# The first weights of a fused attention and FFN kernel, loaded as rows of 1024 columns

## The chip, the cores and the metric

The kernel runs on one core of a Trainium2 chip. The core has TensorE (PE in the profile), VectorE (DVE), ScalarE (ACT), GpSimd (POOL) and SyncE (SP); 16 DMA engines move data between HBM and the on-chip memory SBUF, and matrix products land in the eight banks of PSUM. The metric is the device time of one execution in microseconds (us), as the median of several runs.

## The reference

Eight images of 576 positions, eight heads of 64. Each position sees those at most 32 away; the result of the attention goes through a feed-forward network (FFN) with the tanh form of gelu.

```python
# q, k, v: (8, 8, 576, 64); w_in: (512, 2048); w_out: (2048, 512); all float32
scores = (q @ k.transpose(0, 1, 3, 2)) / sqrt(64)
scores = where(abs(pos[:, None] - pos[None, :]) <= 32, scores, -1e9)
attn = softmax(scores)
x = (attn @ v).transpose(0, 2, 1, 3).reshape(4608, 512)
out = gelu_tanh(x @ w_in) @ w_out                     # (4608, 512)
```

## The kernel before

**Tiling.** The 4608 tokens are worked on as nine tiles of 512 (`t`). For each tile TensorE makes the first product (`ffn_in`): 16 blocks of 128 hidden columns (`n`), each the sum over four row blocks of 128 rows of w_in (`dc`), so 64 matmuls of 128x512 in float16. ACT makes gelu of each block as it leaves PSUM. The second product (`ffn_out`, for tile 0 `ffn_out_0`) sums over the 16 blocks. While tile t is in its products, the attention of image t + 1 is woven into the same instruction streams, step by step, by plans written out by hand (`PLAN_0` for tile 0: at matmul number 4 the scores of group 0, at 9 the turning of pair 1, and so on). Attention is done for pairs of heads (`g`, `pr`): scores, exponential, mask by a band, sums, the product with the values.

**Order.** Nothing is scheduled by a program: each engine runs its instructions in the order in which the kernel's text names them, and waits for semaphores in between. An instruction that waits holds back all that stand behind it on its engine. Loads are issued by SP in the order of the text.

**The beginning.** SP issues q and k of image 0, then its values v by heads (`v_of_pair(g)`: two heads each, 128 KB a head), then w_in, then q and k of image 1 with w_out between them, then the values of image 1. The weights come as float32 and are cast to float16 (`w_in16`, `w_out16`) by DVE, POOL and ACT. They pass through five buffers of 1 MB (`stage`, tag "stage"): the first takes image 0's values, four take w_in, and w_out takes them again one after the other as they come free.

w_in is loaded by quarters of 512 columns (`load_w_in(i, ...)`, L232): a quarter is 1 MB, 4 row blocks of 128 rows, and each row's piece is 512 columns, 2 KB. Quarter 0 comes as two row blocks, then one, then one, with the values of heads 6 and 7 ahead of the last two (L259 to L263); quarters 1 to 3 come as two row blocks each time (L264 to L267).

**Tile 0.** Once the attention of image 0 has its pairs 0 to 2 (`finish`, L815: the product with the values on PE, then a multiplication on DVE, L508, that writes `xT[:, g]`), the first product begins. Row block `dc` of the product needs `xT[:, dc]`, that is pair `dc`, so the fourth pair is finished between row blocks 1 and 2 (L835 to L847): quarter 0's four blocks with row blocks 0 and 1, pair 3, then row blocks 2 and 3. Quarter 0's casts are on POOL (row blocks 0 and 2) and ACT (1 and 3), those of quarters 1 to 3 on DVE (0 and 2) and POOL (1 and 3). Then `quarter(1)`, `quarter(2)` and `quarter(3)` follow (L867 to L882), each row block by row block over its four blocks. A block keeps a PSUM bank from its first matmul to its gelu: blocks 0 to 7 go to the banks D, O, x0, x1, S0 (two halves, each a bank) and S1 (two), and 8 to 15 to the same in turn.

Two smaller pieces stand among these. `band_out` (L307) builds the band mask in six copies on DVE, for use from image 1 on; it stands ahead of `quarter(3, 0, 1)`. `trans_pair(1, 0, ...)` (L881) turns q and k of image 1's first pair by eight transposes on PE, halfway through quarter 3, and copies them out of PSUM: QT on DVE (L357), KT on ACT (L358). After quarter 3 come the casts of w_out's first megabyte (L884: chunk 0 on DVE, 2, 3 and 1 on POOL) and `cast_early(1, 1, ...)` on DVE, and then the second product of tile 0.

Of the kernel before, what the change touches and what calls it, by code (L numbers as in the profile page):

```python
# [9 lines left out]
FP32 = mybir.dt.float32  # L10
FP16 = mybir.dt.float16
# [67 lines left out]
def kernel(  # L79
# [9 lines left out]
    nc = tc.nc  # L89
    B, H, S, D = q.shape  # L90
# [12 lines left out]
    def load_table(which):  # L103
        nc.scalar.add_instruction(mybir.InstLoadActFuncSet(  # L104
            name=nc.get_next_instruction_name(), act_func_set_id=which, ins=[], outs=[]))
# [9 lines left out]
    stage = ctx.enter_context(tc.tile_pool(name="stage", bufs=5))  # L115
    yp = ctx.enter_context(tc.tile_pool(name="yp", bufs=2))
    psM = ctx.enter_context(tc.tile_pool(name="psM", bufs=1, space=PSUM))
    psS = ctx.enter_context(tc.tile_pool(name="psS", bufs=1, space=PSUM))
    psO = ctx.enter_context(tc.tile_pool(name="psO", bufs=1, space=PSUM))
# [11 lines left out]
    w_in16 = big.tile([128, 4, DF], FP16, name="w_in16")  # L131
# [94 lines left out]
    w_in_v = moe_w_in.rearrange("(c p) f -> p c f", p=128)  # L226
    w_out_v = moe_w_out.rearrange("(c p) f -> p c f", p=128)

    def stage_w():
        return stage.tile([128, 4, 512], FP32, name="wst", tag="stage")  # L230

    def load_w_in(i, w, c0=0, c1=4):  # L232
        nc.sync.dma_start(w[:, c0:c1, :], w_in_v[:, c0:c1, 512 * i:512 * i + 512])
        return w

    def load_w_out(i, w, c0=0, c1=4):
        nc.sync.dma_start(w[:, c0:c1, :], w_out_v[:, 4 * i + c0:4 * i + c1, :])
        return w

    def cast_w(w, dst, on_dve=(0, 1), cs=range(4), on_act=()):  # L240
        for c in cs:
            (nc.scalar.copy if c in on_act else nc.vector.tensor_copy if c in on_dve else nc.gpsimd.tensor_copy)(
                dst[:, c, :], w[:, c, :])
# [8 lines left out]
    def v_of_pair(g, hs=(0, 1)):  # L252
        for h in (2 * g + x for x in hs):
            nc.sync.dma_start(raws[0][3][:, :, h, :], v[0, h, 0:512, :].rearrange("(c p) d -> p c d", p=128))  # L254

    vs(4)
    for g in range(3):
        v_of_pair(g)
    wi = [stage_w()]  # L259
    load_w_in(0, wi[0], 0, 2)  # L260
    for x in range(2):
        v_of_pair(3, (x,))
        load_w_in(0, wi[0], 2 + x, 3 + x)  # L263
    for i in range(1, 4):  # L264
        wi.append(stage_w())
        for c0 in (0, 2):
            load_w_in(i, wi[i], c0, c0 + 2)  # L267

    idle = KTs[1][:, 0, 0:512]
    nc.vector.memset(idle, 0.0)  # L270
# [19 lines left out]
    def blocks(copy, dst, src, r, *pieces):  # L290

        for p0, n, w, u in pieces:
            v0 = u + (8 if r == even else 24)
            copy(dst[r, :, p0:p0 + n * w].rearrange("k j (n p) -> k j n p", n=n),
                 src[r, :, v0:v0 + w].rearrange("k j (o p) -> k j o p", o=1).broadcast_to([64, 4, n, w]))
# [11 lines left out]
    def band_out():  # L307
        blocks(nc.vector.tensor_copy, band, full, even, (0, 1, 24, 8), (24, 3, 32, 0), (120, 1, 24, 0))
        blocks(nc.vector.tensor_copy, band, full, odd, (0, 1, 40, -8), (40, 2, 32, 0), (104, 1, 40, 0))
# [36 lines left out]
    def trans_pair(b, pr, pt, ptk=None, now=True, copy=nc.vector.tensor_copy):  # L346
        q16, k16 = halfs[b][0:2]
        ptk = pt[:, 4:8, :] if ptk is None else ptk
        for j in range(4):
            nc.tensor.transpose(pt[:, j, :], q16[:, pr, j, :, :], idn)  # L350
        for j in range(4):
            nc.tensor.transpose(ptk[:, j, :], k16[:, pr, j, :, :], idn)
        if now:
            trans_out(b, pr, pt, ptk, copy)

    def trans_out(b, pr, pt, ptk, copy=nc.vector.tensor_copy):
        nc.vector.tensor_copy(QTs[b][:, pr, :, 0:128], pt[:, 0:4, :])  # L357
        copy(  # L358
            KTs[b % 2][:, pr, :].rearrange("d (p j) -> d p j", j=4),
            ptk[:, 0:4, :].rearrange("d j p -> d p j"))  # L360

    def bank(i):

        return psM.tile([128, 512], FP32, name="mm", tag=f"x{i}")

    def bank16(i):
        return psM.tile([128, 8, 128], FP16, name="pt", tag=f"x{i}")
# [154 lines left out]
    def column(t, n):  # L522

        return n // 2 + 8 * (n % 2) if t else n

    def ffn_in(t, n, d0=0, d1=4, then=True):
        fc = column(t, n)
        if t not in gTs:
            gTs[t] = gp.tile([128, NF, 512], FP16, name="gT", tag="gT")
        if d0 == 0:  # L530
            if t == 0:
                i = n % 8
                if i in (4, 6):
                    phs["S"] = psS.tile([128, 2, 512], FP32, name="ph2", tag=f"S{i // 2 - 2}")
                phs[fc] = psO.tile([128, 512], FP32, name="ph", tag="DO"[i]) if i < 2 else \
                    bank(i - 2) if i < 4 else phs["S"][:, i % 2, :]
            else:
                i = 3 if n in (1, 2) else 0 if n == 0 else (2, 1, 0)[n % 3] if t < NT - 2 else (2, 0)[n % 2 if n > 3 else 0]
                if n == 1:
                    phs["S"] = psS.tile([128, 2, 512], FP32, name="ph3", tag="S0")  # L540
                phs[fc] = bank(i) if i < 2 else phs["S"][:, n - 1, :] if i == 3 else \
                    psO.tile([128, 512], FP32, name="ph", tag="D")
        ph = phs[fc]
        for dc in range(d0, d1):
            nc.tensor.matmul(ph, w_in16[:, dc, fc * 128:fc * 128 + 128],  # L545
                             xT[:, dc, t * 512 % RING:t * 512 % RING + 512],
                             start=(dc == 0), stop=(dc == 3))
        if d1 == 4 and then:
            gelu(t, n)

    def gelu(t, n):
        fc = column(t, n)
        nc.scalar.activation(gTs[t][:, fc, :], phs[fc], AF.Gelu_apprx_tanh)  # L553
        if t and n % 4 == 3:
            sums(t, n // 4)
# [98 lines left out]
    def sums(t, i, which=slice(0, 4)):  # L654

        g, r = gTs[t], slice(2 * i, 2 * i + 2)
        A11, A21, A12, A22 = (g[:, r0 + 2 * i:r0 + 2 * i + 2, c:c + 256]
                              for r0 in (0, 8) for c in (0, 256))
        S1, S2, S3, S4 = (wino[f"S{n}"][:, r, :] for n in (1, 2, 3, 4))
        for dst, x, y, op in ((S1, A21, A22, ALU.add), (S2, S1, A11, ALU.subtract),  # L660
                              (S3, A11, A21, ALU.subtract), (S4, A12, S2, ALU.subtract))[which]:
            nc.vector.tensor_tensor(dst, x, y, op=op)  # L662
# [109 lines left out]
    def pieces(tag, name):  # L772
        return psO.tile([128, 512], FP32, name=name, tag=tag) if tag in "OD" else \
            psS.tile([128, 2, 512], FP32, name=name, tag=tag)[:, 0, :]
# [35 lines left out]
    def values(g, copy):  # L810
        hs = slice(2 * g, 2 * g + 2)
        copy(Vs[0][:, 0:4, hs, :], raws[0][3][:, :, hs, :])
        pair_v(0, nc.vector.tensor_copy, hs)

    def finish(g, o):  # L815
        times(0, g, o, groups.pop((0, g)))
        spread(0, g, o, lts[g])
# [11 lines left out]
    s0 = psS.tile([128, 2, 512], FP32, name="ps_o", tag="S0")  # L829
# [1 line left out]
    sums_of(3)  # L831
    spin(2, 512, s0[:, 1, :])
    values(2, nc.gpsimd.tensor_copy)
    finish(2, s0[:, 0, :])
    nc.gpsimd.tensor_copy(w_in16[:, 0, 0:512], wi[0][:, 0, :])  # L835
    nc.scalar.copy(w_in16[:, 1, 0:512], wi[0][:, 1, :])
    values(3, nc.vector.tensor_copy)
    for dc in range(2):
        for n in range(4):
            ffn_in(0, n, dc, dc + 1)  # L840
    finish(3, pieces("S1", "ps_o"))
    load_table(gelu_set)
    nc.gpsimd.tensor_copy(w_in16[:, 2, 0:512], wi[0][:, 2, :])
    nc.scalar.copy(w_in16[:, 3, 0:512], wi[0][:, 3, :])
    for dc in range(2, 4):
        for n in range(4):
            ffn_in(0, n, dc, dc + 1)  # L847
    cast_w(wi[1], w_in16[:, :, 512:1024], (0, 2))
    cast_w(wi[2], w_in16[:, :, 1024:1536], (0, 2))
    wo.append(load_w_out(1, stage_w()))  # L850
    qk(4)
    tails_0("q")
# [11 lines left out]
    cast_open(1)  # L864
    split = (nc.gpsimd, nc.vector)

    def quarter(i, *dcs):  # L867
        for dc in dcs:
            for n in range(4 * i, 4 * i + 4):
                ffn_in(0, n, dc, dc + 1, then=False)  # L870
        if 3 in dcs:
            for n in range(4 * i, 4 * i + 4):
                gelu(0, n)

    quarter(1, 0, 1, 2, 3)
    cast_w(wi[3], w_in16[:, :, 1536:2048], (0, 2))
    quarter(2, 0, 1, 2, 3)
    cast_early(1, 0, split)
    band_out()
    quarter(3, 0, 1)  # L880
    trans_pair(1, 0, psO.tile([128, 8, 128], FP16, name="pt", tag="D"), bank16(0)[:, 0:4, :], copy=nc.scalar.copy)  # L881
    quarter(3, 2, 3)  # L882
    load_table(exp_set)
    cast_w(wo[0], w_out16[:, 0:4, :], (0,), (0, 2, 3, 1))  # L884
    cast_early(1, 1, (nc.vector, nc.vector))
# [8 lines left out]
    for t in range(NT):  # L894
# [56 lines left out]
        for i in range(113 if t else 65):  # L951
# [8 lines left out]
            for act in plan.get(i, "").split():  # L960
# [18 lines left out]
                elif kind in "np":  # L979
# [7 lines left out]
                    if kind == "n":  # L987
                        n = size(1, g)
# [85 lines left out]
```

## Time and profile before

| | |
|---|---|
| median of 3 runs | 299.17 us (298.62 to 299.78) |
| the profiled execution, its own time | 298.71 us |
| its span, first to last instruction | 297.0 us |
| PE busy | 287.1 us, 97% of the span |
| clock granted to PE | 0.999 of full speed |
| HBM read and written | 36.70 and 9.44 MB |
| w_in: loads and their issues | 4 MB in 9 issues on SP, issued from 11.35 us on |
| w_out: loads and their issues | 4 MB in 6 issues on SP, issued from 21.86 us on |

All places in time are microseconds from the first instruction of the profiled execution. The profile gives a page of totals, and a trace that can be asked for groups of instructions, for waits, for stages, and for each engine's instructions in order of time. A row of the last kind has the start, the duration, the engine, the line of the kernel, what is written from what, and in brackets the idle time before it and what ended it. PE's rows last longer than the distance from one matmul to the next, since matmuls are pipelined; where PE is full, the distance from start to start is what a matmul costs.

### The profile page before, as it was taken

How to read it: one execution, taken by the hardware profiler on the slowest of the kernel's cores; microseconds unless marked ns; L12 is line 12 of the kernel's file. 1: busy time of each engine (PE TensorE's matmuls, PEld its weight loads, DVE VectorE, ACT ScalarE, POOL GpSimd, SP SyncE). 2: the span in 40 equal slices, each digit the busy share in tenths (PEclk: the TensorE clock that was granted, in tenths of full speed). 3: DMA queues.
4: the chain of work that ended last, by engine and by line, in shares of the span. 5: the costliest groups of instructions: out<-in, count | busy, mean ns of one | idle time of the engine just before them, and what ended most of it. 6: DMA issues, size and time to landing. Idle time of an engine off the chain costs nothing.

```text
span 297.0 us, 7282 instructions
## 1 busy us (share of the span) xinstructions
PE 287.1 (97%) x2949; PEld 184.7 (62%) x2949; DVE 209.2 (70%) x466; ACT 196.4 (66%) x315; POOL 89.4 (30%) x141
## 2 busy tenths in 40 slices
PE   7889999999999999999999999999999999999993
PEld 3534444446874587458844884488547867786783
DVE  4662475997986676868686879576966776964772
ACT  4876756778587876678657965695669557705800
POOL 3435415201407731406080606060800050015000
PEclk9999999999999999999999999999999999999999
DMA  7999999989999998989997997999594040004013
GB/s 216 263 297 383 366 280 263 264 178 202 291 192 191 235 233 156 145 167 244 150 193 116 253 145 158 142 227 170 102 175 38 0 116 29 2 13 131 0 35 109
DMA packets 116615, 51.01 MB, mean 172 GB/s; under 512 B 98391, under 2 KB 110167, under 8 KB 116582
## 3 DMA queue, kind: packets, MB, share of 16 engines
q1 hardware_dynamic: 91684, 38.67, 61.6%
q0 software_dynamic: 23776, 10.83, 23.0%
q10 hardware_dynamic: 1122, 1.06, 1.1%
q8 instruction: 23, 0.38, 0.6%
q14 instruction: 10, 0.08, 0.1%
HBM read 36.70 MB, written 9.44 MB: 155 GB/s over the span
## 4 chain that ended last, share of the span: by engine, by line
PE 80%; DMA 13%; DVE 2%; SPq 2%; ACT 1%; issue 1%; POOL 0%
PE mm L719 32%; PE mm L545 17%; PE ph L545 15%; DMA wst<-in_moe_w_out_dram 7%; DMA wst<-in_moe_w_in_dram 5%; PE pu L597 3%; PE ps_s L436 3%; PE ps_d L463 2%; DMA tr<-in_k_dram 2%; PE ps_o L473 2%; SPq L254 2%; PE mm L597 1%; PE ps_od L473 1%; PE ps_od L463 1%; PE mm L691 1%; PE py L719 1%
## 5 line engine op out<-in xcount | busy, mean ns | idle before, releaser
L545 PEld LDWEIGHTS <-w_in 128*128 128x128 f16 x512 | 49.7, 98 | 56.9 <-POOL w_in L835 0.5
L545 PE MATMUL ph<-xT,w_in 128*128 128x512 f16 x256 | 64.1, 379 | 0.4 <-POOL w_in L835 0.4
L545 PE MATMUL mm<-xT,w_in 128*128 128x512 f16 x256 | 64.1, 379 | 0.0
L681 POOL DMA_DIRECT2D out_dram<-y x55 | 32.3, 597 | 83.8 <-DVE y L748 75.5
L553 ACT ACTIVATE gT<-mm 128x512 f16<-128x512 f32 x60 | 35.6, 598 | 33.1 <-PE mm L545 32.5
L719 PEld LDWEIGHTS <-s 128*128 128x128 f16 x512 | 49.3, 98 | 7.1 <-DVE s L662 0.6
L719 PE MATMUL mm<-t,s 128*128 128x256 f16 x376 | 45.2, 273 | 0.3 <-DVE y L732 0.2
L662 DVE TENSOR_TENSOR s<-gT 128x512 f16<-128x512 f16 x64 | 27.2, 426 | 19.0 <-ACT gT L553 18.8
L719 PEld LDWEIGHTS <-gT 128*128 128x128 f16 x384 | 36.2, 98 | 6.5
L553 ACT ACTIVATE gT<-ph 128x512 f16<-128x512 f32 x58 | 32.2, 600 | 10.9 <-PE ph L545 10.9
L449 ACT ACTIVATE pe<-ps_s 128x960 f16<-128x960 f32 (+1 forms) x31 | 29.5, 974 | 13.9 <-PE ps_s L436 13.8
L719 PE MATMUL mm<-w_out,gT 128*128 128x256 f16 x256 | 32.6, 273 | 0.0
L104 ACT ACT_TABLE_LOAD x18 | 23.1, 1283 | 2.2 <-issue 1.9
L498 ACT ACTIVATE lt<-ps_d 128x480 f32<-128x480 f32 (+2 forms) x28 | 15.6, 556 | 10.4 <-PE ps_d L463 6.9
L499 ACT ACTIVATE lt<-lt 128x480 f32<-128x480 f32 (+3 forms) x36 | 21.1, 585 | 1.1
L458 DVE TENSOR_TENSOR pe<-pe,band 128x960 f16<-128x960 f16 x28 | 18.6, 683 | 2.3 <-ACT pe L449 2.3
L473 PEld LDWEIGHTS <-V 128*64 128x64 f16 x520 | 13.8, 111 | 6.3 <-DVE V L218 1.2
L719 PE MATMUL mm<-t,gT 128*128 128x256 f16 x128 | 16.1, 273 | 0.0
L208 POOL DMA_DIRECT2D V<-in_v_dram x16 | 14.3, 909 | 1.1 <-POOL after L953 0.4
L662 DVE TENSOR_TENSOR s<-s,gT 128x512 f16<-128x512 f16 x32 | 13.9, 434 | 1.1
L719 PE MATMUL mm<-w_out,s 128*128 128x256 f16 x120 | 14.6, 273 | 0.0
L508 DVE TENSOR_TENSOR xT<-ps_o,lt 128x480 f16<-128x480 f32 (+5 forms) x26 | 13.4, 536 | 1.1 <-PE ps_o L473 1.1
(146 smaller groups left out, 387.1 us busy)
## 6 DMA issues: line engine op xcount, KB each, us to landing
kr<-in_k_dram SPq DMA_DIRECT2D x31, 256.0 KB, 10.0
qr<-in_q_dram SPq DMA_DIRECT2D x6, 1024.0 KB, 6.9
wst<-in_moe_w_in_dram SPq DMA_DIRECT2D x7, 512.0 KB, 8.4
wst<-in_moe_w_out_dram SPq DMA_DIRECT2D x2, 1024.0 KB, 11.6
wst<-in_moe_w_out_dram SPq DMA_DIRECT2D x4, 512.0 KB, 5.8
qr<-in_v_dram SPq DMA_DIRECT2D x8, 256.0 KB, 5.6
V<-in_v_dram POOLq DMA_DIRECT2D x16, 128.0 KB, 8.8
qr<-in_q_dram SPq DMA_DIRECT2D x7, 256.0 KB, 6.9
```

The source lines that it names most:

```text
L104: nc.scalar.add_instruction(mybir.InstLoadActFuncSet(name=nc.get_next_instruction_name(), act_func_set_id=which, ins=[], outs=[]))
L208: nc.gpsimd.dma_start(V[:, c, :, :], v[b, :, 128 * c:128 * c + 128, :].rearrange("h p d -> p h d"))
L449: nc.scalar.activation(pe, ps[:, :, 0:w], AF.Exp, scale=SCALE)
L458: nc.vector.tensor_tensor(pe, pe, m.rearrange("k (o j) p -> k o j p", o=1).broadcast_to(list(pe.shape)), op=ALU.mult)
L473: nc.tensor.matmul(o[64 * h:64 * h + 64, cols].rearrange("d (j p) -> d j p", j=4)[:, :, p0 - q0:p1 - q0], Vs[b % 2][:, slot, 2 * pr + h, : ...
L498: nc.scalar.activation(lt[:, 0:n], d[:, 0:n], AF.Ln)
L499: nc.scalar.activation(lt[:, 0:n], lt[:, 0:n], AF.Exp, scale=-1.0)
L545: nc.tensor.matmul(ph, w_in16[:, dc, fc * 128:fc * 128 + 128], xT[:, dc, t * 512 % RING:t * 512 % RING + 512], start=(dc == 0), stop=(dc = ...
L553: nc.scalar.activation(gTs[t][:, fc, :], phs[fc], AF.Gelu_apprx_tanh)
L662: nc.vector.tensor_tensor(dst, x, y, op=op)
L681: eng.dma_start(out_v[b, j, q0 + p:q0 + p + e, cols], yo[m:m + e, cols])
L719: nc.tensor.matmul(pys["apart"][:, 0:256] if apart else py[:, blk, :], lhsT, wino[w][:, f, :], start=(new and i % (8 if one else 16) == 0) ...
```

## The change

w_in is loaded as eight pieces of one row block and 1024 columns, so that each of the 128 rows is 1024 columns long, 4 KB. `x` is the half of the columns, `dc` the row block; the order is row blocks 0 and 1 of the left half, with the values of heads 6 and 7 behind the first and the second, then row blocks 2 and 3, and then the right half. Two row blocks share one buffer of 1 MB. The casts are still of 128x512, two to each load: row blocks 0 and 1 of the left half on POOL and ACT, 2 and 3 on POOL and DVE, the right half on DVE and POOL.

The first product of tile 0 follows that order: blocks 0 to 5 with row block 0, then with row block 1, then pair 3 of the attention, then row blocks 2 and 3; then block 6, block 7, blocks 8 to 13 row block by row block, block 14, and block 15. Gelu follows directly on a block's last matmul. Pairs 2 and 3 of the attention leave PE through the two halves of S1, as S0 is now a bank pair of blocks 4 and 5.

`band_out` moves ahead of the casts of the right half. The turned pair moves from the middle of the last quarter to between blocks 14 and 15; its queries now use bank x0 and its keys bank D, and the copy of KT is on DVE in place of ACT.

```diff
+    wi = {}
+
+    def load_w_in(x, dc):
+        if dc % 2 == 0:
+            wi[x, dc // 2] = stage.tile([128, 2, 1024], FP32, name="wst", tag="stage")
+        nc.sync.dma_start(wi[x, dc // 2][:, dc % 2, :], w_in_v[:, dc, 1024 * x:1024 * x + 1024])
+
+    def cast_w_in(x, dc, *copies):
+        for y, copy in enumerate(copies):
+            copy(w_in16[:, dc, 1024 * x + 512 * y:1024 * x + 512 * y + 512],
+                 wi[x, dc // 2][:, dc % 2, 512 * y:512 * y + 512])
...
-    wi = [stage_w()]
-    load_w_in(0, wi[0], 0, 2)
     for x in range(2):
+        load_w_in(0, x)
         v_of_pair(3, (x,))
-        load_w_in(0, wi[0], 2 + x, 3 + x)
-    for i in range(1, 4):
-        wi.append(stage_w())
-        for c0 in (0, 2):
-            load_w_in(i, wi[i], c0, c0 + 2)
+    for x, dc in ((0, 2), (0, 3), (1, 0), (1, 1), (1, 2), (1, 3)):
+        load_w_in(x, dc)
...
     values(2, nc.gpsimd.tensor_copy)
-    finish(2, s0[:, 0, :])
-    nc.gpsimd.tensor_copy(w_in16[:, 0, 0:512], wi[0][:, 0, :])
-    nc.scalar.copy(w_in16[:, 1, 0:512], wi[0][:, 1, :])
+    s1 = psS.tile([128, 2, 512], FP32, name="ps_o", tag="S1")
+    finish(2, s1[:, 0, :])
+    six = range(6)
+
+    def block_in(ns, *dcs):
+        for dc in dcs:
+            for n in ns:
+                ffn_in(0, n, dc, dc + 1)
+
+    cast_w_in(0, 0, nc.gpsimd.tensor_copy, nc.scalar.copy)
     values(3, nc.vector.tensor_copy)
-    for dc in range(2):
-        for n in range(4):
-            ffn_in(0, n, dc, dc + 1)
-    finish(3, pieces("S1", "ps_o"))
+    block_in(six, 0)
+    cast_w_in(0, 1, nc.gpsimd.tensor_copy, nc.scalar.copy)
+    block_in(six, 1)
+    finish(3, s1[:, 1, :])
     load_table(gelu_set)
-    nc.gpsimd.tensor_copy(w_in16[:, 2, 0:512], wi[0][:, 2, :])
-    nc.scalar.copy(w_in16[:, 3, 0:512], wi[0][:, 3, :])
-    for dc in range(2, 4):
-        for n in range(4):
-            ffn_in(0, n, dc, dc + 1)
-    cast_w(wi[1], w_in16[:, :, 512:1024], (0, 2))
-    cast_w(wi[2], w_in16[:, :, 1024:1536], (0, 2))
+    cast_w_in(0, 2, nc.gpsimd.tensor_copy, nc.vector.tensor_copy)
+    cast_w_in(0, 3, nc.gpsimd.tensor_copy, nc.vector.tensor_copy)
+    block_in(six, 2, 3)
+    band_out()
+    for dc in range(4):
+        cast_w_in(1, dc, nc.vector.tensor_copy, nc.gpsimd.tensor_copy)
...
-    quarter(1, 0, 1, 2, 3)
-    cast_w(wi[3], w_in16[:, :, 1536:2048], (0, 2))
-    quarter(2, 0, 1, 2, 3)
+    for n in (6, 7):
+        block_in((n,), 0, 1, 2, 3)
+    block_in(range(8, 14), 0, 1, 2, 3)
     cast_early(1, 0, split)
-    band_out()
-    quarter(3, 0, 1)
-    trans_pair(1, 0, psO.tile([128, 8, 128], FP16, name="pt", tag="D"), bank16(0)[:, 0:4, :], copy=nc.scalar.copy)
-    quarter(3, 2, 3)
+    block_in((14,), 0, 1, 2, 3)
+    pt = psO.tile([128, 8, 128], FP16, name="pt", tag="D")
+    trans_pair(1, 0, bank16(0)[:, 0:4, :], pt[:, 0:4, :])
+    block_in((15,), 0, 1, 2, 3)
```

More of the change, by code (lines that the diff above doesn't have):

```diff
@@ L230, in stage_w @@
         return stage.tile([128, 4, 512], FP32, name="wst", tag="stage")
-    def load_w_in(i, w, c0=0, c1=4):
-        nc.sync.dma_start(w[:, c0:c1, :], w_in_v[:, c0:c1, 512 * i:512 * i + 512])
-        return w
+    wi = {}
[7 more added lines that the diff above has]
+                 wi[x, dc // 2][:, dc % 2, 512 * y:512 * y + 512])
     def load_w_out(i, w, c0=0, c1=4):
@@ L865 @@
     split = (nc.gpsimd, nc.vector)
[L867 to L873, printed above, removed]
-    quarter(1, 0, 1, 2, 3)
-    cast_w(wi[3], w_in16[:, :, 1536:2048], (0, 2))
-    quarter(2, 0, 1, 2, 3)
+    for n in (6, 7):
+        block_in((n,), 0, 1, 2, 3)
+    block_in(range(8, 14), 0, 1, 2, 3)
     cast_early(1, 0, split)
-    band_out()
-    quarter(3, 0, 1)
-    trans_pair(1, 0, psO.tile([128, 8, 128], FP16, name="pt", tag="D"), bank16(0)[:, 0:4, :], copy=nc.scalar.copy)
-    quarter(3, 2, 3)
+    block_in((14,), 0, 1, 2, 3)
+    pt = psO.tile([128, 8, 128], FP16, name="pt", tag="D")
+    trans_pair(1, 0, bank16(0)[:, 0:4, :], pt[:, 0:4, :])
+    block_in((15,), 0, 1, 2, 3)
     load_table(exp_set)
```

## The prediction

> **What bounds the kernel now.** I read the page's busy times first, then the stages, then TensorE's (PE's) waits, then the order of time around each wait.
>
> The page, first part, its line of totals:
>
> ```profile
> PE 287.1 (97%) x2949; PEld 184.7 (62%) x2949; DVE 209.2 (70%) x466; ACT 196.4 (66%) x315; POOL 89.4 (30%) x141
> ```
>
> PE is busy for 287.1 of 297.0 us. The table by stage (PE, PEld, DVE, ACT, POOL busy us and counts; granted clock; DMA share; GB/s) shows where the other 10 us lie:
>
> ```profile
> 10.00:18.00 8.00, 6.47 (x134) 3.50 (x133) 5.17 (x13) 7.55 (x13) 3.66 (x6) 1.00 1.26 256
> 18.00:34.00 16.00, 15.35 (x89) 6.91 (x90) 6.81 (x20) 9.70 (x18) 6.93 (x10) 1.00 1.02 360
> 34.00:47.00 13.00, 12.49 (x129) 5.86 (x130) 7.68 (x16) 9.78 (x16) 4.52 (x7) 1.00 1.11 306
> 47.00:57.00 10.00, 9.49 (x123) 4.78 (x123) 8.22 (x17) 6.86 (x13) 4.92 (x7) 1.00 1.02 259
> 57.00:72.00 15.00, 15.00 (x95) 7.44 (x97) 13.48 (x30) 11.38 (x21) 0.61 (x1) 1.00 1.03 198
> ```
>
> From 57 us on PE stands full, up to the last stage, which the change does not touch. So the whole effect is a shift of PE at about 57 us, made of the few stalls before it. They are in PE's order of time:
>
> ```profile
> 18.06 0.60 PE L545 MATMUL ph<-xT,w_in 128*128 128x512 f16 x2 [0.44 <-POOL w_in L835]
> ...
> 33.96 0.60 PE L691 MATMUL mm<-w_out,gT 128*128 128x512 f16 x2 [0.59 <-DVE w_out L242]
> ...
> 46.92 0.38 PE L691 MATMUL mm<-w_out,gT 128*128 128x512 f16 x1 [0.48 <-POOL w_out L242]
> ...
> 52.85 0.38 PE L691 MATMUL mm<-w_out,gT 128*128 128x512 f16 x1 [0.40 <-POOL w_out L242]
> ```
>
> Every one of them ends with a weight cast that a load released. A 128x512 matmul starts 0.216 us after the one before it, while its row lasts 0.38, so by starts the stalls are 0.62, 0.75, 0.64 and 0.56 us. Between 18.06 and 33.2 PE runs the 64 matmuls of tile 0's first product without a stall over 0.2 us. DVE's order of time gives the landings, since each cast of w_in starts when its load is in:
>
> ```profile
> 21.80 0.43 DVE L242 CAST w_in<-wst 128x512 f16<-128x512 f32 x1 [0.58 <-DMA wst<-in_moe_w_in_dram]
> 23.19 0.43 DVE L242 CAST w_in<-wst 128x512 f16<-128x512 f32 x1 [0.96 <-DMA wst<-in_moe_w_in_dram]
> ...
> 33.48 0.43 DVE L242 CAST w_out<-wst 128x512 f16<-128x512 f32 x1 [1.01 <-DMA wst<-in_moe_w_out_dram]
> ...
> 37.00 0.42 DVE L357 COPY QT<-pt 128x512 f16<-128x512 f16 x1 [1.59 <-PE pt L352]
> 37.34 0.68 DVE L358 COPY KT<-pt 128x512 f16<-128x512 f16 x1
> 37.94 0.80 DVE L242 CAST w_out<-wst 128x512 f16<-128x512 f32 x1
> ```
>
> The reader is to see that PE's first product, once begun, waits for nothing: the casts stay ahead of it, and the stream of loads sets 33.96, 46.92 and 52.85.
>
> **The change, part by part.** Times are of the profiled execution (298.71 us with a span of 297.0, 0.46 below the median of 299.17).
>
> *Loads.* 4 MB of w_in go as 1024 packets of 4 KB in place of 2048 of 2 KB; one issue on SP's queue (about 0.5 us, nine become eight) goes. The packet records have 18 ns for 256 B, 46 for 1 KB, 86 for 2 KB; 4 KB exists only in stores, at 159. By that, 2048 x 86 less 1024 x 159 is 13.3 us of packet time, over 16 engines 0.8 us, about 0.1 per 512 KB. Ends: none (time by bytes alone), and 1.0 (4.19 MB at 440 GB/s, what the best slices of 0.3 us moved, against 400). I take 0.8 by the nearest row. The stream moved about 400 GB/s from 21 to 24 us, so nothing here caps it at less. The Trainium skill ("DMA: Bandwidth & Descriptors", Specifications) speaks against this term: it puts line rate at 512 B and more and a core's share of HBM at about 358 GB/s, by which 2 KB rows would already run as fast as 4 KB ones; the sum would then be the first rival's. The rows above, past that share and with a cost for each packet, do not agree with it.
>
> In the built program each SP load waits for the one issued eight before it. Everything behind w_in (q and k of image 1, w_out) moves one place, and the bytes in flight stay the same.
>
> *What a byte buys.* Before, the first 512 KB gave eight matmuls and the first 1 MB sixteen; now six and twelve, as six blocks fit into PSUM. The landings by bytes: the first load at 17.3 as now; the next 640 KB (second load and head 7's v) ended at 19.9 (ACT's cast of row block 3 starts at 19.93), so the second load comes at 19.35 and v at 19.8; then 21.5, 22.75 and on, a tenth more ahead each time, up to 28.4 for the last in place of 29.26, and w_out's first at 32.65.
>
> *PE.* Six matmuls 18.0 to 19.3. The second load's cast (POOL and ACT, 0.61 and 0.62, side by side) ends at 20.0: stall 0.75. Six to 21.35; values of the fourth pair, 0.45, to 21.8 (v lands 19.8, cast 0.47 and two copies 0.57 on DVE, done by 20.9). Third block: POOL's cast ends 22.15, stall 0.4. DVE's half of it stands behind the multiplication L508 (0.69), which waits for those values until 21.9; with a cast of 0.43 it is there at 23.0, when PE wants it. Fourth: lands 22.75, POOL's cast takes up to 0.87 beside DVE (0.61 alone): stall 0.2. All 24 are done at 25.0. Blocks 6 and 7 take 1.73, blocks 8 to 13 5.19 (their loads are 1 us or more ahead, and ACT's gelus, 0.54 apart from 24.1, free the six banks by 27.4; the last is wanted at 27.8), block 14 0.87: 32.75. The turned pair takes 0.45, block 15 0.87: PE is free at 34.05. So the new stalls are 1.35 us; ends are 0 (loads early) and 2.7 (one straggler, below).
>
> *The turned pair.* ACT's copy of KT (0.58, hidden among gelus) goes to DVE (0.68, 0.60 apart from its follower), ahead of the cast of w_out's first chunk, which PE waits for. Queries are turned at 33.0 and readable at 33.2; QT's copy occupies 0.34, KT's 0.60, the cast 0.43: 34.65. PE starts w_out at 34.70 in place of 33.96: +0.74. Behind that cast DVE has only q and k of pair 1, wanted over 1 us later. The landing of w_out at 32.65 no longer decides, nor would 33.45.
>
> *Band mask.* Six copies (0.90 on DVE) go ahead of the casts of w_in's second half: 23.45 to 24.35. The first of those casts ends at 24.8 and PE wants it at 26.7, so it is hidden; without that cover it would cost 0.4. Before, it kept QT's copy waiting to 32.04, on no path.
>
> *Nothing for the rest.* Casts stay 16 (ACT 2, DVE 6, POOL 8), matmuls and gelus the same; ACT ends its gelus at 35.3 against 35.0 and reaches the first exponential 0.2 later, used only at 38.1.
>
> *Sum.* PE would reach the load that now stops it at 46.92 without that stall at 46.29, so now at 47.03: the landing, 0.8 earlier, is past, and the shift falls to +0.1. At 52.85 the stall of 0.56 goes too, but what is late next is DVE's V copies, which free the values at 53.62: they hang on the scores at 48.97 through ACT and the mask, and so carry the +0.1. 298.71 + 0.1 is 298.8; on the median, 299.3.
>
> **The rivals.** *Landings stay as they are (packets cost by bytes).* Then 24 matmuls end at 25.4, w_out starts at 35.1, and 1.15 less 0.64 leaves +0.5: 299.7. For it: 1 KB to 2 KB saves only 6 of 92 ns.
>
> *Faster: the lull goes.* Between 17.4 and 18.8 us packets of 2 KB took up to 1.5 us, and the us from 18 moved 118 GB/s. If that does not recur, loads are 1 us earlier on top; the second and third blocks wait 0.4 in all, w_out starts at 33.9 (-0.06), and the stalls of 0.64 and 0.56 vanish with the stream 1.8 ahead: -0.7, 298.5. Against it: nothing says that the lull is chance. No more is to be had than all stalls, 1.9 to 2.0 us, and the V copies keep at least half.
>
> *Slower: one straggling DMA engine.* Of the first load's 16 pieces 15 landed by 15.98 and the last at 17.34, 1.36 us later, after an instruction fetch of 1.28 us on a DMA engine. Before, w_in had over 1 us to spare past the first load; now PE takes each row block as it lands. If the second load is hit so, w_out starts at 36.06: 2.1 less 0.64 is +1.46, 300.6. It is slower as soon as w_out starts later than 34.6, and measurably from 36.1, a second load at 20.75 or later.
>
> *The change does not do what it says:* its rows could still be cut into 2 KB packets; that is the first rival's price.
>
> **How the numbers follow.** The forecast 0.39, with its own range 298.9 to 299.7; landings unchanged 0.15; lull gone 0.20; straggler 0.16; 0.10 for something else. A measurement here tells about 0.5% (1.5 us) from no change: under 297.7 is faster, over 300.7 slower. Forecast and unchanged landings lie inside. Of the lull's chance a quarter passes the line, where the first load too escapes its straggler and PE starts up to 0.6 before 18.06; of the straggler's a bit over half (two such hits, or one with unchanged landings, +1.9). The rest falls mostly outside, 0.04 below and 0.06 above. Faster 0.09, same 0.76, slower 0.15. The range 297.8 to 300.9 leaves out about 0.2: the outermost part of the two outer cases and of the rest.
>
> **What would show it.** Packets of 4096 B on the load queue at about 160 ns, 1024 of them; in PE's waits, first-product lines released by w_in casts of POOL (new, some 1.3 us in all); at about 34.7 a wait on DVE's cast of w_out with KT's copy just ahead of it; no stall, or under 0.2, at 47. Wrong if PE is full from 18 to 34 after all, if the wait for w_out is ended by a landing, or if PE shows stalls past 57 us.

## The result, and the profile after

The changed kernel takes 303.94 us (median of six runs, 302.33 to 305.14) against 299.53 us for the kernel before in the same comparison: a ratio of 1.0148, with a 95% interval from 1.0121 to 1.0175. It is 4.4 us slower, where 299.3 us had been forecast. Its profiled execution took 303.29 us with a span of 301.6.

The table by stage of the changed kernel (columns as before: PE, PEld, DVE, ACT, POOL busy, granted clock, DMA share, GB/s) shows the place of the loss:

```profile
10.00:18.00 8.00, 6.42 (x133) 3.37 (x125) 4.84 (x13) 7.41 (x11) 3.68 (x6) 1.00 1.21 276
18.00:34.00 16.00, 12.64 (x70) 5.30 (x71) 6.92 (x18) 6.51 (x11) 7.43 (x11) 1.00 1.04 386
34.00:47.00 13.00, 10.95 (x95) 5.34 (x94) 6.65 (x13) 8.72 (x14) 3.31 (x5) 1.00 1.14 287
47.00:57.00 10.00, 9.93 (x108) 4.41 (x107) 7.13 (x16) 6.81 (x13) 3.74 (x6) 1.00 1.00 254
```

From 18 to 34 us PE is busy 12.64 us in place of 15.35, from 34 to 47 us 10.95 in place of 12.49; before 18 us it stands as it did, and from 47 us on it is busier than it was (9.93 us in place of 9.49). Memory is not short: 386 GB/s in the second row, where it was 360. PE's waits from 18 to 40 us, by who ended them (total, times, longest):

```profile
PE ph L549 <- ACT gT L557: 4.5, 4, 1.8
PE ph L549 <- POOL w_in L241: 0.6, 2, 0.3
PE ph L549 <- DVE w_in L241: 0.5, 1, 0.5
```

Four waits for gelu (L557, ACT) are there that were not in the profile before, and they are four fifths of all. The two other lines are waits for row blocks of w_in. Of POOL's two, the one at 18.06 us was there before (0.44 us, now 0.29) and the one at 19.84 is new, as the prediction had it; DVE's, at 23.18, is new as well, where the prediction had that cast come in time. PE's order of time shows where the four stand:

```profile
24.06 0.59 PE L549 MATMUL mm<-xT,w_in 128*128 128x512 f16 x2
24.49 0.38 PE L549 MATMUL ph<-xT,w_in 128*128 128x512 f16 x1
26.65 1.24 PE L549 MATMUL ph<-xT,w_in 128*128 128x512 f16 x5 [1.78 <-ACT gT L557]
28.57 1.46 PE L549 MATMUL ph<-xT,w_in 128*128 128x512 f16 x6 [0.69 <-ACT gT L557]
...
34.18 0.38 PE L549 MATMUL ph<-xT,w_in 128*128 128x512 f16 x1
36.34 1.24 PE L549 MATMUL ph<-xT,w_in 128*128 128x512 f16 x5 [1.78 <-ACT gT L557]
...
38.26 1.02 PE L549 MATMUL ph<-xT,w_in 128*128 128x512 f16 x4 [0.24 <-ACT gT L557]
39.25 0.60 PE L695 MATMUL mm<-w_out,gT 128*128 128x512 f16 x2
```

By starts (a matmul's distance is 0.216 us) the waits are 1.94, 0.85, 1.94 and 0.40 us, 5.13 together. The first holds back a single matmul: the one at 24.49 is block 4's last, and at 26.65 comes block 5's last, followed by the four of block 6. Block 5 had everything it needs. What it waits for is seen in ACT's order of time:

```profile
24.04 1.08 ACT L557 ACTIVATE gT<-ph 128x512 f16<-128x512 f32 x2 [2.99 <-PE ph L549]
25.01 1.09 ACT L557 ACTIVATE gT<-mm 128x512 f16<-128x512 f32 x2
25.97 0.63 ACT L557 ACTIVATE gT<-ph 128x512 f16<-128x512 f32 x1
27.06 0.60 ACT L557 ACTIVATE gT<-ph 128x512 f16<-128x512 f32 x1 [0.47 <-PE ph L549]
27.92 0.60 ACT L557 ACTIVATE gT<-ph 128x512 f16<-128x512 f32 x1 [0.27 <-PE ph L549]
```

These are the gelus of blocks 0 and 1, 2 and 3, then 4 (to 26.60), 5 and 6. Block 5's last matmul begins 0.05 us after the gelu of block 4 has ended. The two blocks are halves of one PSUM tile (tag S0). In the text of the changed kernel the gelu of block 4 stands between block 4's last matmul and block 5's, and block 5's last matmul waits for a semaphore of ACT. Blocks 6 and 7, 12 and 13, 14 and 15 share tiles likewise, and theirs are the other three waits; for 7 and 15 it is the block's first matmul that is held, since block 6 or 14 stands ahead of it whole, with its gelu.

In the kernel before, all gelus of quarters 1 to 3 stood behind the matmuls of their quarter, and no matmul had to wait for the gelu of its tile's other half. In quarter 0 they stood directly behind each block there too, but its four blocks have a tile each.

w_out's product so starts at 39.25 in place of 33.96, 5.29 us late; the landings then stop PE no more at 47 us (the stall of 0.64 is gone), and the span ends 4.6 us later. The stall of 0.56 that was at 53 us gives nothing back: two waits of 0.15 and 0.37 us, at 57.69 and 59.18, stand in its place.

### The profile page after: what moved, and what is told of

Same layout as the page of the kernel before. It is cut to its first block, busy times and chain, and to the rows that moved or that the text cites. A ratio compares the mean times of both kernels' runs of the same rounds, so it can differ in the third digit from the quotient of the medians.

```text
span 301.6 us, 7281 instructions
## 1 busy us (share of the span) xinstructions
PE 287.4 (95%) x2949; PEld 184.6 (61%) x2949; DVE 210.6 (70%) x467; ACT 196.3 (65%) x314; POOL 88.4 (29%) x141
## 4 chain that ended last, share of the span: by engine, by line
PE 86%; DMA 4%; ACT 3%; DVE 2%; SPq 2%; issue 1%; POOL 0%; DVEq 0%
PE mm L723 32%; PE ph L549 18%; PE mm L549 18%; PE ps_s L440 3%; PE pu L601 3%; DMA wst<-in_moe_w_in_dram 2%; PE mm L695 2%; PE ps_d L467 2%; ACT gT L557 2%; PE py L695 2%; PE ps_o L477 2%; SPq L262 2%; DMA tr<-in_k_dram 2%; PE mm L601 1%; PE ps_od L467 1%
## 5 line engine op out<-in xcount | busy, mean ns | idle before, releaser
L549 PE MATMUL ph<-xT,w_in 128*128 128x512 f16 x256 | 64.9, 379 | 5.6 <-ACT gT L557 4.5
L557 ACT ACTIVATE gT<-mm 128x512 f16<-128x512 f32 x60 | 35.6, 598 | 33.1 <-PE mm L549 32.5
L557 ACT ACTIVATE gT<-ph 128x512 f16<-128x512 f32 x58 | 32.9, 600 | 16.3 <-PE ph L549 16.3
```

## The experiments

The theory formed from this is the *shared pair*: a gelu that stands in the text between the matmuls of two blocks in one PSUM tile makes the second block's next matmul wait for it, at a price set by that gelu's place in ACT's queue. Its first rival is the *bank count*: six blocks at a time use up the banks, and gelu frees them too late wherever it stands.

### Gelus behind their group

```diff
     def block_in(ns, *dcs):
         for dc in dcs:
             for n in ns:
-                ffn_in(0, n, dc, dc + 1)
+                ffn_in(0, n, dc, dc + 1, then=False)
+
+    def gelus(ns):
+        for n in ns:
+            gelu(0, n)
...
     block_in(six, 2, 3)
+    gelus(six)
...
     for n in (6, 7):
         block_in((n,), 0, 1, 2, 3)
+    gelus((6, 7))
     block_in(range(8, 14), 0, 1, 2, 3)
+    gelus(range(8, 14))
...
     block_in((15,), 0, 1, 2, 3)
+    gelus((14, 15))
```

> The changed kernel with the gelus of tile 0 behind the matmuls of their group (0 to 5, 6 and 7, 8 to 13, 14 and 15) and no other edit. Theory (shared pair: a block's last matmul is held until the gelu of the other half of the same PSUM tile has read it, because the gelu now stands between them in the text): TensorE's four waits for gelu (1.94, 0.85, 1.94 and 0.40 us by starts) go, w_out starts at about 34.65 in place of 39.25, the stall at 47 absorbs 0.64 of what is left, and the time is that of the kernel before within 0.3 us (about 4.5 us under the changed kernel). Rival (bank count: six blocks at a time use up the banks and gelu frees them too late, wherever it stands in the text): the waits move to the first matmuls of blocks 6 and 8 to 13 and the time stays 4 us or more above the kernel before.

298.35 us against 299.56, a ratio of 0.9965 with an interval from 0.9945 to 0.9986: not only back, but a little faster than the kernel before. The medians are 1.2 us apart, where at most 0.3 was expected; the spans of the profiled executions differ by 0.3 (296.7 and 297.0). PE's waits from 18 to 36 us, and two places in its order of time:

```profile
PE ph L549 <- POOL w_in L241: 0.6, 2, 0.3
PE ph L549 <- DVE w_in L241: 0.4, 1, 0.4
PE mm L695 <- DVE w_out L250: 0.4, 1, 0.4
```

```profile
24.65 2.75 PE L549 MATMUL ph<-xT,w_in 128*128 128x512 f16 x12
...
34.69 0.60 PE L695 MATMUL mm<-w_out,gT 128*128 128x512 f16 x2 [0.36 <-DVE w_out L250]
```

The gelus are gone from the waits; blocks 4 to 7 run in one row of twelve matmuls where two waits stood. w_out starts at 34.69, where 34.65 was expected. The bank count falls: with the same banks and the same six blocks nothing waits for a bank.

### Only the order within each pair

```diff
-                ffn_in(0, n, dc, dc + 1)
+                ffn_in(0, n, dc, dc + 1, then=n % 8 not in (4, 6))
+                if dc == 3 and n % 8 in (5, 7):
+                    gelu(0, n - 1)
```

> The changed kernel with one edit: the gelu of blocks 4, 6, 12 and 14 stands behind that of their neighbour in the same PSUM tile (5, 7, 13, 15); all others stay directly behind their block's last matmul. Shared-pair theory: that is all of it; w_out starts at 34.7 within 0.3, as with all gelus behind, and the time is about 298.4 (4.5 to 5.5 us under the changed kernel). Rival (what matters is that gelus come in bursts of six): the waits stay, 303.

298.62 us against 299.54 (0.9966, 0.9944 to 0.9988), with w_out at 34.54. Every other gelu stands where the changed kernel has it, so the place of four gelus, each now put behind its neighbour's, is the whole loss. The rival, gelus in bursts of six, falls: the bursts are still there.

### The kernel before, with the gelus moved

```diff
     def quarter(i, *dcs):
         for dc in dcs:
             for n in range(4 * i, 4 * i + 4):
-                ffn_in(0, n, dc, dc + 1, then=False)
-        if 3 in dcs:
-            for n in range(4 * i, 4 * i + 4):
-                gelu(0, n)
+                ffn_in(0, n, dc, dc + 1)
```

> The kernel before, with each gelu of blocks 4 to 15 directly behind its block's last matmul, as in the changed kernel; loads, order of matmuls and casts as before. Theory (shared pair): blocks 5, 7, 13 and 15 wait for the gelus of 4, 6, 12 and 14, about 0.86 and 1.16 us in each of the two quarters, 4.0 in all; w_out starts at about 37.2, 0.64 is absorbed at 47, and the kernel is 2.6 us slower than before (1.5 to 3.5). Rival (bank count, or the order of loads): nothing is added, within 0.3 us of the kernel before.

301.15 us against 299.56 (1.0057, 1.0032 to 1.0082): 1.6 to 1.7 us slower, without any of the change's loads or orders. Its PE in order of time:

```profile
25.82 0.59 PE L545 MATMUL ph<-xT,w_in 128*128 128x512 f16 x2 [0.69 <-ACT gT L553]
27.37 0.81 PE L545 MATMUL ph<-xT,w_in 128*128 128x512 f16 x3 [0.96 <-ACT gT L553]
...
35.13 0.59 PE L545 MATMUL ph<-xT,w_in 128*128 128x512 f16 x2 [0.69 <-ACT gT L553]
36.68 0.38 PE L545 MATMUL ph<-xT,w_in 128*128 128x512 f16 x1 [0.96 <-ACT gT L553]
```

By starts the waits are 0.85, 1.12, 0.85 and 1.12 us, where 0.86 and 1.16 were expected, in quarters 1 and 3 alone; quarter 2, whose four blocks have a bank each to themselves, has none. The loss is 1 us less than the 2.6 us expected, though within the range given. Of 3.94 us of waits 1.9 reached the end of the profiled execution (298.9 against a span of 297.0). w_out starts at 36.90 in place of 33.96, 2.94 us late, so 1.0 us is taken up there, mostly by the stall of 0.75; the stall at 47 us takes up 0.64. At 53 us, where the kernel before has its stall of 0.56, two waits of 0.16 us are left, and tile 1's first product begins at 58.03 in place of 56.06, 1.97 us late. The stall at 53 us had not been reckoned with.

### The pair taken apart in the order

```diff
-            for n in ns:
+            for n in ((*ns[4:5], *ns[0:4], *ns[5:6]) if dc == 3 and len(ns) == 6 else ns):
                 ffn_in(0, n, dc, dc + 1)
```

> The changed kernel with gelus still directly behind each block, but in the last row block of the groups of six the order is 4, 0, 1, 2, 3, 5 (and 12, 8, 9, 10, 11, 13): the first half's gelu is then first in ScalarE's queue. Theory (the price of the wait is the place of the gelu in ScalarE's queue, one gelu each 0.49 us against one matmul each 0.216): the two waits of 1.94 us go, but the queue is no shorter, so that block 7 and block 15 wait longer (1.3 to 1.8 in place of 0.85 and 0.40); w_out starts near 37.2 in place of 39.25, 2 us gained of the 4.6 lost. Rival (bank count): no gain, as the banks come free no earlier.

303.77 us (two runs; 1.014, 1.0107 to 1.0173): the time is not what was expected, the waits nearly are. Total, times and longest from 18 to 40 us:

```profile
PE ph L549 <- ACT gT L557: 2.5, 2, 1.7
...
PE pt L354 <- ACT gT L557: 0.2, 1, 0.2
```

By starts they are 1.84 (block 7), 0.38 (the turned pair) and 1.03 (block 15), 3.25 in place of 5.13: the two waits of 1.94 are gone, 1.9 us are gained, and the queue makes itself felt one block later, as expected (1.3 to 1.8 had been said for block 7 and for block 15; the latter has 1.41 with the turned pair's part). w_out starts at 38.56 all the same, where 37.2 was expected, because the first product began late and slowly in this execution. The row from 17 to 21 us, and under it that of the changed kernel:

```profile
17.00:21.00 4.00, 4.00 (x27) 1.59 (x27) 1.63 (x4) 2.67 (x5) 1.29 (x2) 0.57 0.96 311
17.00:21.00 4.00, 3.03 (x26) 1.31 (x26) 1.99 (x6) 2.82 (x4) 1.28 (x3) 1.00 1.03 358
```

The granted clock is 0.57 in the place of 1.00. The product's first matmul stands at 18.90 in place of 18.06, and the first ones stood 0.43 us apart. The loads were late as well: POOL's cast of the third row block begins at 22.97 in place of 20.95, and PE waits 0.53 us for it. So 0.7 us are left of the 1.9 at w_out's start. They are lost at 137.51, where PE waits 0.92 us for a transposing DMA (KT from k), which it does in no other profiled execution. This run speaks by its waits, not by its time.

### KT's copy back on ACT

```diff
-    trans_pair(1, 0, bank16(0)[:, 0:4, :], pt[:, 0:4, :])
+    trans_pair(1, 0, bank16(0)[:, 0:4, :], pt[:, 0:4, :], copy=nc.scalar.copy)
```

This and the two last experiments start from the kernel with the gelus behind their group.

> The first experiment's kernel (gelus behind) with the copy of KT of the turned pair back on ScalarE. Theory of the prediction: VectorE's cast of w_out's first chunk then starts 0.6 us earlier, w_out starts at about 34.05 in place of 34.65, and since loads are now ahead and no stall waits at 47, 0.5 to 0.6 us remain: 0.5 us under the kernel before. Rival (the copy is hidden): same as the first experiment.

299.12 us (0.9986, 0.9953 to 1.0019): no gain, rather 0.8 us more than without the edit, though the two intervals overlap. On the spot it did what was said. DVE in order of time, with the cast of w_out next behind QT's copy and PE no longer waiting for it:

```profile
32.29 0.42 DVE L361 COPY QT<-pt 128x512 f16<-128x512 f16 x1 [2.35 <-PE pt L354]
32.63 0.52 DVE L250 CAST w_out<-wst 128x512 f16<-128x512 f32 x1
```

w_out started at 33.21, where 34.05 was expected (0.62 of the 1.48 us gained there came from an earlier start of the product), and PE's last matmul began at 291.03 in place of 291.88. The span is 296.9 us in place of 296.7 all the same: the stores behind the last matmul took 1 us longer in this execution. Why the gain did not show in the median either is open.

### The loads alone

```diff
     values(2, nc.gpsimd.tensor_copy)
     finish(2, s0[:, 0, :])
-    nc.gpsimd.tensor_copy(w_in16[:, 0, 0:512], wi[0][:, 0, :])
-    nc.scalar.copy(w_in16[:, 1, 0:512], wi[0][:, 1, :])
+    cast_w_in(0, 0, nc.gpsimd.tensor_copy, nc.scalar.copy)
     values(3, nc.vector.tensor_copy)
+    cast_w_in(0, 1, nc.gpsimd.tensor_copy, nc.scalar.copy)
...
-    nc.gpsimd.tensor_copy(w_in16[:, 2, 0:512], wi[0][:, 2, :])
-    nc.scalar.copy(w_in16[:, 3, 0:512], wi[0][:, 3, :])
+    cast_w_in(0, 2, nc.gpsimd.tensor_copy, nc.vector.tensor_copy)
+    cast_w_in(0, 3, nc.gpsimd.tensor_copy, nc.vector.tensor_copy)
```

(on the kernel before, with the changed kernel's loads and the casts of the right half as there)

> The kernel before with the new loads and their casts alone: order of the product by quarters, gelus, band mask and turned pair as before. Theory (a first product by four blocks takes 0.87 us a row block, a load brings one in 1.3 to 1.8, so PE waits for row blocks 1 to 3, some 1.9 us in all, later given back by landings that come 1.5 us earlier): w_out starts at about 34.6, the stall of 0.64 at 47 is gone, the time is that of the kernel before within 0.5 us. Rival (longer rows are worth their 1.5 us wherever the product is not held by gelus): 1 us or more under the kernel before.

300.17 us against 299.54 (1.0027, 1.0003 to 1.0052): 0.6 to 0.8 us slower, a little past what was expected. The rival, 1 us or more of gain from longer rows, falls for these loads in the order in which they come here. The profiled execution was one with the clock at 0.63 from 17 to 21 us, so its places in time (w_out at 37.27, where 34.6 was expected) are not compared.

### The same with rows of 2 KB

```diff
-            wi[x, dc // 2] = stage.tile([128, 2, 1024], FP32, name="wst", tag="stage")
-        nc.sync.dma_start(wi[x, dc // 2][:, dc % 2, :], w_in_v[:, dc, 1024 * x:1024 * x + 1024])
+            wi[x, dc // 2] = stage.tile([128, 2, 2, 512], FP32, name="wst", tag="stage")
+        nc.sync.dma_start(wi[x, dc // 2][:, :, dc % 2, :],
+                          w_in_v[:, dc, 1024 * x:1024 * x + 1024].rearrange("p (y c) -> p y c", y=2))
```

> The first experiment's kernel (gelus behind) with every load's rows cut into two pieces of 2 KB (the two halves of a row in different places of the buffer), order and bytes of loads as they are. If longer packets save 0.1 us per 512 KB as the prediction has it, the load of w_out's first megabyte lands 0.8 us later than in the first experiment, the row blocks wait 0.1 to 0.3 us longer, and the time is 0.1 to 0.4 us more. If packets cost by bytes, landings and time are those of the first experiment.

299.09 us (0.9984, 0.9958 to 1.001) against 298.35 with rows of 4 KB; runs of both overlap widely. The packets answer better than the time: 2048 of 2 KB with a median of 85 ns here, 1024 of 4 KB at 159 ns there. POOL's casts start as loads land; the last four of this kernel's w_in, and then those of the changed kernel:

```profile
26.54 0.64 POOL L242 CAST w_in<-wst 128x512 f16<-128x512 f32 x1 [0.48 <-DMA wst<-in_moe_w_in_dram]
27.89 0.87 POOL L242 CAST w_in<-wst 128x512 f16<-128x512 f32 x1 [0.71 <-DMA wst<-in_moe_w_in_dram]
29.25 0.87 POOL L242 CAST w_in<-wst 128x512 f16<-128x512 f32 x1 [0.49 <-DMA wst<-in_moe_w_in_dram]
30.63 0.87 POOL L242 CAST w_in<-wst 128x512 f16<-128x512 f32 x1 [0.51 <-DMA wst<-in_moe_w_in_dram]
```

```profile
22.23 0.62 POOL L241 CAST w_in<-wst 128x512 f16<-128x512 f32 x1 [0.66 <-DMA wst<-in_moe_w_in_dram]
23.51 0.68 POOL L241 CAST w_in<-wst 128x512 f16<-128x512 f32 x1 [0.66 <-DMA wst<-in_moe_w_in_dram]
24.80 0.83 POOL L241 CAST w_in<-wst 128x512 f16<-128x512 f32 x1 [0.61 <-DMA wst<-in_moe_w_in_dram]
26.07 0.87 POOL L241 CAST w_in<-wst 128x512 f16<-128x512 f32 x1 [0.44 <-DMA wst<-in_moe_w_in_dram]
27.45 0.87 POOL L241 CAST w_in<-wst 128x512 f16<-128x512 f32 x1 [0.52 <-DMA wst<-in_moe_w_in_dram]
```

512 KB land every 1.36 us (4.09 over three) with 2 KB rows and every 1.28 with 4 KB rows (from 22.23 to 26.07, 3.84 over three; the last step is 1.38 in both). That is 0.08 us per 512 KB, some 0.6 for all of w_in, as an estimate from two executions. Others are less even: the kernel with the gelus behind has steps of 1.28, 1.28, 1.76 and 1.21 us, and the kernel before, with 2 KB rows, three of 1.38 or 1.39, one of 1.29 and one of 2.02. In the time the gain is not shown. The whole stream of this execution lies 2 to 3 us later, but that came with its first loads (the second was cast from 21.5 us on, from 19.4 in the kernel that it starts from), in a stretch in which the DMA engines moved 130 to 340 GB/s from 13 to 20 us, and is not laid to the rows.

### Row blocks 2 and 3 on ACT

```diff
-    cast_w_in(0, 2, nc.gpsimd.tensor_copy, nc.vector.tensor_copy)
-    cast_w_in(0, 3, nc.gpsimd.tensor_copy, nc.vector.tensor_copy)
+    cast_w_in(0, 2, nc.gpsimd.tensor_copy, nc.scalar.copy)
+    cast_w_in(0, 3, nc.gpsimd.tensor_copy, nc.scalar.copy)
```

> The first experiment's kernel (gelus behind) with the second halves of row blocks 2 and 3 cast on ScalarE in place of VectorE, where they stand behind the multiplication that waits for pair 3. Theory: PE's wait of 0.61 us for that cast at 23 us goes, w_out starts 0.6 us earlier (34.1), no load stops PE later, and the time is 0.4 to 0.6 us under the first experiment, about 297.8. Rival (as the copy of KT moved to ScalarE: PE gets ahead but the time stays): within 0.2 us of the first experiment or above it.

298.88 us (0.9985, 0.9955 to 1.0016), 0.5 us above the 298.35 of the kernel that it starts from, with overlapping intervals: no gain in time, as the rival had it. On the spot it did what was said: PE's wait for that cast is gone, and from the values of pair 3 to w_out PE takes 12.58 us (22.72 to 35.30), where it took 13.21 (21.48 to 34.69). That w_out starts at 35.30, and not at the expected 34.1, comes from a late start: this execution had the clock at 0.58 from 17 to 21 us, and its product began at 19.75 in place of 18.28. Why the 0.6 us do not show in the median is open, as with KT's copy.

Of the versions run, the one with the gelus behind their group has the lowest median. It is ahead of both kernels; from the one with only the pairs swapped (298.62) it is not told apart.

## Why the prediction was wrong

The step that failed is the clause on PE that ACT's gelus "free the six banks by 27.4", with the line that has "matmuls and gelus the same". It put the wait of matmuls for gelus at nothing. The gelus were priced as work on ACT and as releasers of banks for the next blocks. That the change also moves them in the text, from behind a quarter's matmuls to directly behind each block (for blocks 4 to 15), was described and not priced, and what is queued behind the wait that it adds was not asked. Blocks 4 and 5 were taken for two banks; for the program's waits they are one tile. The four waits measured 5.13 us.

With them put in, the prediction's own sum comes out. The first three, 4.73 us, stand ahead of the turned pair and move PE and DVE's cast of w_out alike. The fourth, 0.40, falls into the time in which PE would have waited for that cast, whose row in the changed kernel is

```profile
38.78 0.42 DVE L250 CAST w_out<-wst 128x512 f16<-128x512 f32 x1
```

It ends at 39.20, 0.08 us after block 15's matmuls have gone through (four from 38.26). The waits for row blocks came to 0.18 us less than said. So the predicted start of w_out, 34.70, becomes 39.25, which is where it is, and the predicted +0.1, from which the 0.64 at 47 us had been taken already, becomes about +4.6; measured were 4.6 in the spans and 4.4 in the medians.

The other steps, by the changed kernel and by the one with the gelus behind:

- *Loads.* Packets of 4096 B at 159 ns, as taken. The saving by load is 0.08 us in place of 0.10, by the estimate above. The landings were earlier still than by that: w_out's first megabyte is cast by POOL from 31.69 on, where 32.65 was said and 33.5 was before, because the lull was milder (no packet of the loads over 0.6 us around 17 to 19 us, where one took 1.5). So part of the rival "the lull goes" came true, and bought nothing.
- *Waits for row blocks.* 0.75, 0.4 and 0.2 were said, 1.35 together; the changed kernel has 0.48 and 0.69, together 1.17, the second for DVE's half of the third row block behind the multiplication of pair 3.
- *Turned pair.* With the gelus out of the way, w_out starts at 34.69 (34.70 said), released by DVE's cast behind KT's copy. That the two agree so closely is in part luck: the product began at 18.28 where 18.0 was said, and its waits for row blocks came to 1.11 us in place of 1.35.
- *The stall at 47 us takes up 0.64.* 5.29 at w_out's start became 4.6 at the end: right. Of the V copies only part held: with the gelus behind, PE is at tile 1's first product at 55.82 against 56.06 before, 0.24 ahead where +0.1 was said.
- *The straggling DMA engine,* the rival on the slow side, did not come: the second load was cast from 19.17 on, 19.35 said.

So the forecast of about 299 us belongs to a kernel that differs from the changed one by the place of four gelus. That one measures 298.6, and 298.4 with all gelus behind. Why these are 0.7 to 0.9 us under the forecast is not shown: the spans of their profiled executions are 296.8 and 296.7, only 0.2 and 0.3 under the 297.0 of the kernel before.

## What to carry to other kernels

When a change moves an instruction in the text of a kernel whose waits follow from that text, price the waits it makes for others, not only its own time: here four gelus of 0.6 us, on the same engine as before, cost 4.6 us by standing between matmuls of one PSUM tile. Read the built program's waits of the changed kernel against those of the old before pricing anything else; a wait of the bounding engine that is new there needs its own line in the sum. And a consumer that drains slower than the producer fills (0.49 us a gelu, 0.216 a matmul) makes such a wait longer the later it stands in the consumer's queue: a gelu that was fifth in the queue cost 1.94 us, one that found ACT idle 0.85.

## What the runs showed of the hardware that was not expected

In three profiled executions (the pair taken apart, the loads alone, row blocks on ACT) the granted clock was 0.57 to 0.63 from 17 to 21 us and 1.00 in the stretch after it; the profiles of the other kernels show 1.00 in that place. In finer windows it is 0.50 for some 3.4 us (from 17.4 us, 16.6 and 16.9), each time after 10.2 us at 1.00. While it was halved, PE's 128x512 matmuls stood 0.43 us apart in place of 0.216. PE's busy time from 10 to 17 us does not tell these executions from the others: 5.34, 5.29 and 4.60 us, but 5.20 with rows of 2 KB, where the clock stayed at 1.00. What sets the clock back just there is open.
